# The last step of a fused window-attention and rational-activation kernel: other parts, other engines for its linear terms, another order

## The chip, the cores and the metric

The kernel runs on one core of a Trainium2 chip. The core has engines that run side by side and wait for each other by semaphores: TensorE (PE) multiplies matrices into PSUM, VectorE (DVE) and ScalarE (ACT) work element by element, GpSimd (POOL) and SyncE (SP) here mostly issue DMAs. The metric is the device time of one execution in microseconds (us); lower is better.

## The reference

Attention over a sliding window with four sink keys, then a feed-forward block whose activation is a ratio of polynomials:

```python
scores = scale * q @ k.T                       # 4 batches, 8 heads, 768 rows, 64 wide
keep = is_sink | in_window                     # first 4 keys, or the last 128
x = softmax(where(keep, scores, -1e9)) @ v     # -> 3072 rows, 512 wide
h = x @ w_in                                   # 512 -> 2048
P = a[0] + a[1] * h + a[2] * h2 + a[3] * h3
Q = 1.0 + abs(b[0]) * abs(h) + abs(b[1]) * h2
out = (P / (Q + 1e-06)) @ w_out                # 2048 -> 512
```

## The kernel before

The 3072 rows are worked off in 12 steps of 256 rows (step 0 to 11). In each step TensorE computes scores (`scores`), ScalarE exponentiates them out of PSUM (`exps`), TensorE multiplies with v (`attend`), VectorE divides by the sums (`normalize`), the result is turned (`turn_x`), and the feed-forward part follows on a tile of 128 partitions x 4096 columns: 16 blocks of 128 ff channels ("ff blocks") lie side by side, 256 columns each.

The feed-forward part of a step is made of these pieces, with their lines in the profile:

- `gemm1` (PE, L767): four groups of 4 ff blocks, 16 matmuls each, into a PSUM bank pair called ps_h, ps_o, ps_m; a table `BANK` says which. `copy_in` (ACT, L774) copies a group to hb in bf16 and frees the bank.
- `sqa` / `sqd`: the square (ACT L781 or DVE L783); `and` (DVE L788): the absolute value by a bit mask; `den` (DVE L792): their sum.
- `ln` (ACT L811) and `exp` (ACT L816): the reciprocal of the denominator as exp(-ln). `ln` takes its scale and its bias from one value per partition (`qsc`, `one_eps`).
- `even` (DVE L797): a2*sq + a0; `odd` (DVE L801): a3*sq + a1, in place; `odd_h` (DVE L805): times h; `num` (DVE L808): even + odd_h; `gate` (DVE L821): num times the reciprocal, the input of the second projection.
- `gemm2` (PE, L829): 16 ff blocks x 2 row halves of 128x512 matmuls. `copy_out` (ACT L838; in the last step one half on ACT L567 and one on DVE L569) copies the sums out, `store` (L844, L846) writes them by DMA. Step 10 and those before are stored in one DMA of 512 KB from SP's queue, the last step in two of 256 KB, from ACT's queue and from SP's.

Steps 1 to 10 do the elementwise pieces on all 4096 columns at once. The last step does them in four equal parts of 4 ff blocks (1024 columns), each part with its own two groups of 4 second-projection matmuls, so that TensorE can begin before all of the tile is done. Every engine works off its instructions in the order in which they are written. That order comes from a list of piece numbers, `ORDER`; a negative number there is `spin`, which multiplies a tile of ones on TensorE to no use: `spin(n)` issues n/4 matmuls of 512 columns and the rest as matmuls of 128. `-3` stands before the first scores of step 0.

Of the kernel before, what the change touches and what calls it, by code (L numbers as in the profile page):

```python
# [12 lines left out]
AF = mybir.ActivationFunctionType  # L13
ALU = mybir.AluOpType
# [3 lines left out]
ORDER = [  # L18
# [43 lines left out]
def kernel(  # L62
# [13 lines left out]
    nc = tc.nc  # L76
# [26 lines left out]
    X_PE = 5  # L103
    PARTS0 = 4
    V_PE = 3
    HOLD_X = tuple(range(8))
    HOLD_H = tuple(range(7))
    KB = 3
# [68 lines left out]
             ('gemm1', 9, 1): 'ps_m',  # L177
             ('gemm1', 9, 2): 'ps_o',
             ('gemm1', 9, 3): 'ps_h',
             ('gemm1', 10, 0): 'ps_o',  # L180
             ('gemm1', 10, 1): 'ps_m',
             ('gemm1', 10, 2): 'ps_o',
             ('gemm1', 10, 3): 'ps_m',
             ('gemm1', 11, 0): 'ps_m',
             ('gemm1', 11, 2): 'ps_m',
             ('gemm1', 11, 3): 'ps_m',
             ('gemm2', 6, 0, 0): 'ps_m',
             ('gemm2', 9, 0, 0): 'ps_o',
             ('scores', 0, 0): 'ps_h',
             ('scores', 0, 1): 'ps_m',  # L190
             ('scores', 0, 3): 'ps_m',
# [86 lines left out]
    a0, a1, a2, a3 = (acoef[:, n:n + 1] for n in range(4))  # L278
# [481 lines left out]
    LAST = NSTEP - 1  # L760
# [30 lines left out]
    def denominator(m, c):  # L791
        nc.vector.tensor_tensor(out=den[m][:, c], in0=den[m][:, c], in1=sq[m][:, c], op=ALU.add)  # L792

    def even(m, c):
        if m not in num:
            num[m] = m_sb.tile([P, MW], BF16, tag="num", name="num", bufs=1)
        nc.vector.tensor_scalar(out=num[m][:, c], in0=sq[m][:, c], scalar1=a2, scalar2=a0,  # L797
                                op0=ALU.mult, op1=ALU.add)

    def odd(m, c):  # L800
        nc.vector.tensor_scalar(out=sq[m][:, c], in0=sq[m][:, c], scalar1=a3, scalar2=a1,  # L801
                                op0=ALU.mult, op1=ALU.add)

    def odd_h(m, c):
        nc.vector.tensor_tensor(out=sq[m][:, c], in0=sq[m][:, c], in1=hb[m][:, c], op=ALU.mult)  # L805
# [317 lines left out]

    early_casts = [("cast_k0", 0), ("cast_k0", 1)]

    def cut(n, k_):
        return slice(k_ * MW // n, (k_ + 1) * MW // n)

    def parts(m):
        return 4 if m == LAST else PARTS0 if m == 0 else 1  # L1130

    def every(nm, m):
        return [(nm, m, p_) for p_ in range(parts(m))] if m >= 0 else []
# [1 line left out]
    for m in range(NSTEP):  # L1135
# [15 lines left out]
        if m in HOLD_H:  # L1151
            piece(("hold", "h", m), "POOL", 0.2, r_ + 4, lambda m=m: hold("h", m),
                  [("copy_in", m, j) for j in range(4)])
        w_ = MW // np_
        for p_ in range(np_):
            c = cut(np_, p_)
            js = range(p_ * 4 // np_, (p_ + 1) * 4 // np_)
            ins = [("copy_in", m, j) for j in js]
            d_ = 4.0 * p_ / np_ if np_ > 1 else 3.0
            q_ = 1.2 if m == LAST else 2.5  # L1160
            piece(("and", m, p_), "DVE", on_dve(w_, 4), r_ + d_ + 1.2, lambda m=m, c=c: magnitude(m, c),
                  ins + every("gate", old)
                  + ([("turn_%sc" % w_, s_, g_) for s_ in (1, 2) for w_ in "kq"
                      for g_ in halves(s_, w_)] if m == 1 else []))
            if np_ == 1:
                k_ = SQ_ACT.get(m, 2)
                x_ = k_ * GW
                if k_:
                    piece(("sqa", m, p_), "ACT", on_act(x_), r_ + 3.9,
                          lambda m=m, x_=x_: square(m, slice(0, x_), "act"),  # L1170
                          ins[:k_] + (every("num", old) or early_casts))
                if k_ < 4:
                    piece(("sqd", m, p_), "DVE", on_dve(MW - x_, 2), r_ + 4.25,
                          lambda m=m, x_=x_: square(m, slice(x_, MW), "dve"),
                          ins[k_:] + (every("num", old) or early_casts))
            else:
                eng = "act" if m == LAST or p_ == 0 else "dve"
                nm = "sqa" if eng == "act" else "sqd"
                on = {"act": ("ACT", on_act(w_)), "dve": ("DVE", on_dve(w_, 2))}[eng]
                piece((nm, m, p_), on[0], on[1], r_ + d_ + 1.3,  # L1180
                      lambda m=m, c=c, eng=eng: square(m, c, eng),
                      ins + (every("num", old) or early_casts))
            sqs = [("sqa", m, p_) if ("sqa", m, p_) in work else None,
                   ("sqd", m, p_) if ("sqd", m, p_) in work else None]
            piece(("den", m, p_), "DVE", on_dve(w_, 2), r_ + d_ + 1.4,
                  lambda m=m, c=c: denominator(m, c), [("and", m, p_)] + sqs)
            piece(("ln", m, p_), "ACT", on_act(w_, 0.3), r_ + d_ + 1.8, lambda m=m, c=c: log_den(m, c),
                  [("den", m, p_), ("scalars",)] + every("exp", m - 1))
            piece(("exp", m, p_), "ACT", on_act(w_, 0.2), r_ + d_ + 2.8,
                  lambda m=m, c=c: recip_den(m, c), [("ln", m, p_)])  # L1190
            piece(("even", m, p_), "DVE", on_dve(w_, 3.25), r_ + d_ + 2.6, lambda m=m, c=c: even(m, c),
                  sqs + [("scalars",)]
                  + (every("gate", m - 1) or [("cast_q0", 0), ("cast_q0", 1)]))
            piece(("odd", m, p_), "DVE", on_dve(w_, 3.4), r_ + d_ + 2.8, lambda m=m, c=c: odd(m, c),
                  [("even", m, p_), ("den", m, p_)])
            piece(("odd_h", m, p_), "DVE", on_dve(w_, 2), r_ + d_ + 3.0, lambda m=m, c=c: odd_h(m, c),
                  [("odd", m, p_)])
            piece(("num", m, p_), "DVE", on_dve(w_, 2), r_ + d_ + 3.2,
                  lambda m=m, c=c: numerator(m, c), [("odd_h", m, p_)])
            piece(("gate", m, p_), "DVE", on_dve(w_, 2), r_ + d_ + (3.4 if m == LAST else 6.0),  # L1200
                  lambda m=m, c=c: gate(m, c),
                  [("num", m, p_), ("exp", m, p_)]
                  + ([("gemm2", m - 2, tt, 1) for tt in range(NTS)] if m >= 2 else
                     [("turn_k0", 0), ("turn_k0", 1), ("turn_q0", 0), ("turn_q0", 1)]))
        n2 = 4 if m == LAST else 2
        for tt in range(NTS):
            if m == LAST or tt == 0:
                home = bank_of(("gemm2", m, tt, 0), "ps_m" if m == LAST and tt == 0 else "ps_h")
            for part in range(n2):
                f0, f1 = part * NFFC // n2, (part + 1) * NFFC // n2  # L1210
                gates = [("gate", m, p_) for p_ in range(np_)
                         if p_ * NFFC // np_ < f1 and (p_ + 1) * NFFC // np_ > f0]
                piece(("gemm2", m, tt, part), "PE", 3.48 / n2,
                      (r_ + 10.6 + 2 * tt + part) if m < LAST else (r_ + 8 + part + 0.5 * tt),
                      lambda m=m, tt=tt, f0=f0, f1=f1, home=home: project_out(m, tt, f0, f1, home),
                      gates + [("load_w_out", c) for c in range(f0 * 4 // NFFC, (f1 * 4 + NFFC - 1) // NFFC)]
                      + ([("gemm2", m, tt, part - 1)] if part else [("gemm2", m, 0, 0)] if tt and m < LAST else []),
                      takes=home if part == 0 and (tt == 0 or m == LAST) else None)
# [49 lines left out]
```

## Time and profile before

| | |
|---|---|
| median of 3 runs | 242.64 us (241.71 to 242.86) |
| the profiled execution, its own time | 240.56 us |
| span of the profiled execution, first to last instruction | 238.9 us |
| TensorE busy | 216.1 us, 90% |
| VectorE busy | 215.2 us, 90% |
| ScalarE busy | 210.1 us, 88% |
| GpSimd busy | 92.7 us, 39% |

The time of a run holds some 1.7 us around the span (240.56 less 238.9). All starts below count from the start of the span. Three engines are busy for about nine tenths of it, so no share of busy time alone says which one sets the end; that is read from the waits in each stretch.

### The profile page before, as it was taken

What the parts mean: (1) busy time and instruction counts of PE and PEld (TensorE: products, weight loads), DVE (VectorE), ACT (ScalarE), POOL (GpSimd) and SP (SyncE); (2) the same over time, 40 slices, a digit from 0 to 9 for tenths busy, and PEclk for the clock granted to TensorE, in tenths of its full rate; (3) what the DMA queues carried; (4) which work ended last, traced back from release to release, by engine and by line L of the source; (5) the groups of instructions that cost most, each with busy time, mean ns of one, the idle gap of its engine ahead of it and who ended that gap; (6) DMA issues with size and microseconds to landing.
All of it is one profiled execution on the core that took longest, in us unless ns stands there. A gap on an engine that the chain in (4) does not pass through costs nothing.

```text
span 238.9 us, 7308 instructions
## 1 busy us (share of the span) xinstructions
PE 216.1 (90%) x3229; PEld 146.8 (61%) x3249; DVE 215.2 (90%) x253; ACT 210.1 (88%) x172; POOL 92.7 (39%) x126
## 2 busy tenths in 40 slices
PE   0497898995999999999999999999999999999993
PEld 0365676784874757746578658568647768545431
DVE  3678299999799999898999999999999999999991
ACT  2357799997899998999999899999999999999960
POOL 8914409597939880499910980000000000000000
PEclk9999999999999999999999999999999999999999
DMA  6999999999999999799994999570305110004222
GB/s 186 166 178 137 202 170 79 125 134 128 164 185 147 137 162 150 208 98 77 141 129 89 158 89 73 140 125 26 25 3 198 25 25 0 1 3 170 93 88 88
DMA packets 95375, 26.98 MB, mean 113 GB/s; under 512 B 86128, under 2 KB 92272, under 8 KB 95344
## 3 DMA queue, kind: packets, MB, share of 16 engines
q0 software_dynamic: 65024, 12.98, 84.8%
q1 hardware_dynamic: 28792, 12.61, 28.4%
q10 hardware_dynamic: 1528, 0.93, 1.4%
q8 instruction: 25, 0.41, 0.8%
q14 instruction: 6, 0.05, 0.1%
HBM read 27.30 MB, written 6.29 MB: 141 GB/s over the span
## 4 chain that ended last, share of the span: by engine, by line
PE 52%; ACT 24%; DVE 7%; DMA 6%; issue 4%; POOL 4%; SPq 2%; ACTq 0%; POOLq 0%; DVEq 0%
PE ps_h L829 18%; PE ps_o L767 9%; PE ps_m L767 8%; ACT lnq L811 6%; ACT hb L774 5%; ACT den L816 4%; DMA kT<-k_bf 4%; PE ps_m L829 3%; ACT sq L781 3%; ACT e L667 3%; PE ps_h L767 2%; DMA v<-in_v_dram 2%; PE ps_m L708 2%; PE ps_s L647 1%; SPq L602 1%
## 5 line engine op out<-in xcount | busy, mean ns | idle before, releaser
L767 PEld LDWEIGHTS <-w_in_sb 128*128 128x128 bf16 x768 | 73.7, 98 | 14.8 <-issue 3.5
L829 PE MATMUL ps_h<-w_out_sb,g 128*128 128x512 bf16 x287 | 68.2, 379 | 1.9 <-issue 1.0
L829 PEld LDWEIGHTS <-g 128*128 128x128 bf16 x384 | 36.6, 98 | 42.0 <-DVE g L821 1.6
L811 ACT ACTIVATE lnq<-den,one_eps,qsc 128x4096 f32<-128x4096 bf16 (+1 forms) x18 | 48.2, 2678 | 0.0
L816 ACT ACTIVATE den<-lnq 128x4096 bf16<-128x4096 f32 (+1 forms) x18 | 44.8, 2491 | 0.2
L767 PE MATMUL ps_m<-xblk,w_in_sb 128*128 128x256 bf16 x352 | 42.1, 273 | 0.6 <-ACT hb L774 0.3
L767 PE MATMUL ps_o<-xblk,w_in_sb 128*128 128x256 bf16 x336 | 40.2, 273 | 0.0
L381 POOL DMA_DIRECT2D v<-in_v_dram x48 | 36.1, 765 | 0.1
L808 DVE TENSOR_TENSOR num<-num,sq 128x4096 bf16<-128x4096 bf16 (+1 forms) x18 | 28.3, 1578 | 0.2
L821 DVE TENSOR_TENSOR g<-num,den 128x4096 bf16<-128x4096 bf16 (+1 forms) x18 | 28.3, 1574 | 0.1
L805 DVE TENSOR_TENSOR sq<-sq,hb 128x4096 bf16<-128x4096 bf16 (+1 forms) x18 | 28.3, 1576 | 0.1
L792 DVE TENSOR_TENSOR den<-den,sq 128x4096 bf16<-128x4096 bf16 (+1 forms) x18 | 28.2, 1574 | 0.1
L774 ACT ACTIVATE hb<-ps_o 128x1024 bf16<-128x1024 f32 x21 | 21.8, 1038 | 3.3 <-PE ps_o L767 3.2
L774 ACT ACTIVATE hb<-ps_m 128x1024 bf16<-128x1024 f32 x22 | 22.9, 1039 | 0.6 <-PE ps_m L767 0.5
L667 ACT ACTIVATE e<-ps_s 128x768 bf16<-128x768 f32 (+1 forms) x25 | 22.1, 885 | 0.0
L781 ACT ACTIVATE sq<-hb 128x1024 bf16<-128x1024 bf16 (+1 forms) x15 | 20.1, 1355 | 0.1
L797 DVE TENSOR_SCALAR num<-sq,acoef 128x4096 bf16<-128x4096 bf16 (+1 forms) x18 | 18.3, 1024 | 0.4 <-ACT sq L781 0.3
L801 DVE TENSOR_SCALAR sq<-sq,acoef 128x4096 bf16<-128x4096 bf16 (+1 forms) x18 | 17.9, 999 | 0.2
L783 DVE TENSOR_TENSOR sq<-hb 128x2048 bf16<-128x2048 bf16 (+2 forms) x13 | 16.9, 1300 | 1.0 <-ACT hb L774 0.9
L708 PEld LDWEIGHTS <-e 64*64 64x64 bf16 x1216 | 13.1, 107 | 5.4 <-issue 4.4
L343 POOL DMA_DIRECT2D q_bf<-in_q_dram x15 | 14.8, 988 | 3.7 <-DMA w_out_sb<-in_moe_w_out_dram 3.5
L788 DVE TENSOR_SCALAR den<-hb 128x2048 uint32<-128x2048 uint32 (+1 forms) x18 | 16.1, 896 | 0.0
(136 smaller groups left out, 265.8 us busy)
## 6 DMA issues: line engine op xcount, KB each, us to landing
out_dram<-o_t SPq DMA_DIRECT2D x11, 512.0 KB, 3.0
w_in_sb<-in_moe_w_in_dram POOLq DMA_DIRECT2D x4, 512.0 KB, 10.8
k_bf<-in_k_dram POOLq DMA_DIRECT2D x16, 128.0 KB, 6.2
w_out_sb<-in_moe_w_out_dram POOLq DMA_DIRECT2D x4, 512.0 KB, 8.8
q_bf<-in_q_dram POOLq DMA_DIRECT2D x15, 128.0 KB, 6.2
v<-in_v_dram POOLq DMA_DIRECT2D x24, 64.0 KB, 5.8
stage_v<-in_v_dram POOLq DMA_DIRECT2D x3, 256.0 KB, 9.8
v<-in_v_dram POOLq DMA_DIRECT2D x24, 32.0 KB, 5.0
```

What stands on the lines that cost most here:

```text
L381: nc.gpsimd.dma_start(out=v_fix[b % 2][half(r), g * NHF:(g + steps) * NHF, hl, 0:D], in_=v[b, h, g * TS:(g + steps) * TS, :].rearrange("(j ...
L667: nc.scalar.activation(out=data, in_=ps[:, :, c0:512], func=AF.Exp, scale=inv_sqrt_d)
L767: nc.tensor.matmul(ps[:, n, :], lhsT=w_in_all[:, c, fc * P:(fc + 1) * P], rhs=xblk[m][:, c, :], start=(c == 0), stop=(c == NDMC - 1))
L774: nc.scalar.activation(out=hb[m][:, j * GW:(j + 1) * GW], in_=ps_h.pop((m, j)).rearrange("p n c -> p (n c)"), func=AF.Copy)
L781: nc.scalar.activation(out=sq[m][:, c], in_=hb[m][:, c], func=AF.Square)
L792: nc.vector.tensor_tensor(out=den[m][:, c], in0=den[m][:, c], in1=sq[m][:, c], op=ALU.add)
L805: nc.vector.tensor_tensor(out=sq[m][:, c], in0=sq[m][:, c], in1=hb[m][:, c], op=ALU.mult)
L808: nc.vector.tensor_tensor(out=num[m][:, c], in0=num[m][:, c], in1=sq[m][:, c], op=ALU.add)
L811: nc.scalar.activation(out=lnq_fix[:, c], in_=den[m][:, c], func=AF.Ln, scale=qsc, bias=one_eps)
L816: nc.scalar.activation(out=den[m][:, c], in_=lnq_fix[:, c], func=AF.Exp, scale=-1.0)
L821: nc.vector.tensor_tensor(out=g_of[m][:, c], in0=num[m][:, c], in1=den[m][:, c], op=ALU.mult)
L829: nc.tensor.matmul(ps_out[own][:, tt, :], lhsT=g_of[m][:, co:co + P], rhs=w_out_all[:, fc, :], start=(fc == 0), stop=(fc == NFFC - 1))
```

## The change

The last step is cut into parts of 5, 5, 4 and 2 ff blocks (1280, 1280, 1024 and 512 columns) in place of 4, 4, 4 and 4, for the elementwise pieces and for the second projection alike. For its last two parts the two linear terms, `even` and `odd`, are no longer a VectorE multiply-add but a ScalarE activation with the function Identity, whose scale and bias are the same one value per partition. Some PSUM banks of steps 9 to 11 are exchanged. `ORDER` is another one from the first projection of step 11 on, and the spin at the start is 7 in place of 3.

```diff
 ORDER = [
 ...
-    130, 178, -3, 182, 150, 184, 183, 131, 185, 120, 151, 132, 24, 186, 152, 180, 18, 187, 181, 17,
+    130, 178, -7, 150, 182, 184, 183, 131, 120, 151, 185, 132, 24, 186, 152, 180, 18, 187, 181, 17,
...
+    LAST_FC = (5, 5, 4, 2)
+    TERMS_ACT = (("even", 2), ("odd", 2), ("even", 3), ("odd", 3))
...
-    def even(m, c):
+    def linear(eng, out, in_, slope, shift):
+        if eng == "ACT":
+            nc.scalar.activation(out=out, in_=in_, func=AF.Identity, scale=slope, bias=shift)
+        else:
+            nc.vector.tensor_scalar(out=out, in0=in_, scalar1=slope, scalar2=shift, op0=ALU.mult,
+                                    op1=ALU.add)
+
+    def even(m, c, eng="DVE"):
         if m not in num:
             num[m] = m_sb.tile([P, MW], BF16, tag="num", name="num", bufs=1)
-        nc.vector.tensor_scalar(out=num[m][:, c], in0=sq[m][:, c], scalar1=a2, scalar2=a0,
-                                op0=ALU.mult, op1=ALU.add)
-
-    def odd(m, c):
-        nc.vector.tensor_scalar(out=sq[m][:, c], in0=sq[m][:, c], scalar1=a3, scalar2=a1,
-                                op0=ALU.mult, op1=ALU.add)
+        linear(eng, num[m][:, c], sq[m][:, c], a2, a0)
+
+    def odd(m, c, eng="DVE"):
+        linear(eng, sq[m][:, c], sq[m][:, c], a3, a1)
...
+    def ff_cut(m, n, k_):
+        if m == LAST:
+            return sum(LAST_FC[:k_]), sum(LAST_FC[:k_ + 1])
+        return k_ * NFFC // n, (k_ + 1) * NFFC // n
```

Up to the first `gemm1` group of step 11 the engines run the same instructions in the same order as before, the spin excepted. Then, on TensorE, the four `gemm1` groups of step 11 stand in one row ahead of the second projections of steps 8 and 9; before, two of the four stood among those. On SP's queue the stores of steps 7, 8 and 9 are exchanged. The last instructions of ScalarE change as follows. Before, the place is from the second `copy_out` from the end on (L838 on ps_o is that of step 9, on ps_h that of step 10; L811 is `ln`, L816 `exp`, 1024 columns a part):

```order
L838 ACTIVATE o_t<-ps_o 128x1024
L816 ACTIVATE den<-lnq 128x1024
L811 ACTIVATE lnq<-den,one_eps,qsc 128x1024
L816 ACTIVATE den<-lnq 128x1024
L838 ACTIVATE o_t<-ps_h 128x1024
L811 ACTIVATE lnq<-den,one_eps,qsc 128x1024
L816 ACTIVATE den<-lnq 128x1024
L567 ACTIVATE o_t<-ps_m 128x512
L844 DMA out_dram<-o_t 128x512
```

In the changed kernel, from the `ln` of the second part on (the lines are 7 higher: L818 is `ln`, L823 `exp`, L845 `copy_out` of step 10; L798 is the new Identity):

```order
L818 ACTIVATE lnq<-den,one_eps,qsc 128x1280
L798 ACTIVATE sq<-sq,acoef 128x1024
L823 ACTIVATE den<-lnq 128x1280
L818 ACTIVATE lnq<-den,one_eps,qsc 128x1024
L823 ACTIVATE den<-lnq 128x1024
L798 ACTIVATE sq<-sq,acoef 128x512
L818 ACTIVATE lnq<-den,one_eps,qsc 128x512
L823 ACTIVATE den<-lnq 128x512
L845 ACTIVATE o_t<-ps_h 128x1024
L569 ACTIVATE o_t<-ps_o 128x512
L851 DMA out_dram<-o_t 128x512
```

Step 10's `copy_out` has moved from before the last `ln` to behind the last `exp`, directly ahead of the last step's own `copy_out`, and the two `odd` terms stand among the last `ln` and `exp`. On VectorE the end before was this, from the `odd` of the third part on (L801 `odd`, L805 `odd_h`, L797 `even`, L808 `num`, L821 `gate`):

```order
L801 TENSOR_SCALAR sq<-sq,acoef 128x1024
L821 TENSOR_TENSOR g<-num,den 128x1024
L805 TENSOR_TENSOR sq<-sq,hb 128x1024
L797 TENSOR_SCALAR num<-sq,acoef 128x1024
L808 TENSOR_TENSOR num<-num,sq 128x1024
L801 TENSOR_SCALAR sq<-sq,acoef 128x1024
L821 TENSOR_TENSOR g<-num,den 128x1024
L805 TENSOR_TENSOR sq<-sq,hb 128x1024
L808 TENSOR_TENSOR num<-num,sq 128x1024
L821 TENSOR_TENSOR g<-num,den 128x1024
L569 COPY o_t<-ps_h 128x512
```

In the changed kernel, from the `odd_h` of the second part on (L812 `odd_h`, L815 `num`, L828 `gate`):

```order
L812 TENSOR_TENSOR sq<-sq,hb 128x1280
L815 TENSOR_TENSOR num<-num,sq 128x1280
L828 TENSOR_TENSOR g<-num,den 128x1280
L812 TENSOR_TENSOR sq<-sq,hb 128x1024
L815 TENSOR_TENSOR num<-num,sq 128x1024
L828 TENSOR_TENSOR g<-num,den 128x1024
L812 TENSOR_TENSOR sq<-sq,hb 128x512
L815 TENSOR_TENSOR num<-num,sq 128x512
L828 TENSOR_TENSOR g<-num,den 128x512
L571 COPY o_t<-ps_m 128x512
```

Each part now runs through in one piece, `odd_h`, `num`, `gate`, with no linear term between them.

## Rows read from the trace of the kernel before

**Rows 1.** The page: busy time and its share of the span.

```profile
PE 216.1 (90%) x3229; PEld 146.8 (61%) x3249; DVE 215.2 (90%) x253; ACT 210.1 (88%) x172; POOL 92.7 (39%) x126
```

**Rows 2.** Timeline of TensorE, last 20 us: start, us, instruction, [idle before, releaser].

```profile
219.96 7.07 PE L829 MATMUL ps_h<-w_out_sb,g 128*128 128x512 bf16 x31
227.18 1.04 PE L829 MATMUL ps_m<-w_out_sb,g 128*128 128x512 bf16 x4
228.41 1.02 PE L829 MATMUL ps_h<-w_out_sb,g 128*128 128x512 bf16 x4 [0.20 <-ACT o_t L838]
...
233.08 1.04 PE L829 MATMUL ps_h<-w_out_sb,g 128*128 128x512 bf16 x4 [0.19 <-DVE g L821]
233.95 1.03 PE L829 MATMUL ps_m<-w_out_sb,g 128*128 128x512 bf16 x4
```

**Rows 3.** Timeline of ScalarE and its DMA queue, last 27 us.

```profile
212.83 3.62 ACT L816 ACTIVATE den<-lnq 128x4096 bf16<-128x4096 f32 x1
216.35 1.00 ACT L838 ACTIVATE o_t<-ps_h 128x1024 f32<-128x1024 f32 x1
...
218.16 1.06 ACT L781 ACTIVATE sq<-hb 128x1024 bf16<-128x1024 bf16 x1
219.11 1.24 ACT L811 ACTIVATE lnq<-den,one_eps,qsc 128x1024 f32<-128x1024 bf16 x1
220.24 1.05 ACT L781 ACTIVATE sq<-hb 128x1024 bf16<-128x1024 bf16 x1
...
227.36 1.00 ACT L838 ACTIVATE o_t<-ps_h 128x1024 f32<-128x1024 f32 x1
228.26 1.23 ACT L811 ACTIVATE lnq<-den,one_eps,qsc 128x1024 f32<-128x1024 bf16 x1
229.53 1.06 ACT L816 ACTIVATE den<-lnq 128x1024 bf16<-128x1024 f32 x1
235.02 0.60 ACT L567 ACTIVATE o_t<-ps_m 128x512 f32<-128x512 f32 x1 [4.43 <-PE ps_m L829]
235.65 0.36 ACTq L844 DMA_DIRECT2D out_dram<-o_t  x1
```

**Rows 4.** Timeline of VectorE, the last step.

```profile
220.53 1.00 DVE L797 TENSOR_SCALAR num<-sq,acoef 128x1024 bf16<-128x1024 bf16 x2
...
232.33 0.69 DVE L821 TENSOR_TENSOR g<-num,den 128x1024 bf16<-128x1024 bf16 x1
234.16 0.69 DVE L569 COPY o_t<-ps_h 128x512 f32<-128x512 f32 x1 [1.13 <-PE ps_h L829]
```

**Rows 5.** Timeline of SP's queue, last 13 us: the stores of steps 10 and 11.

```profile
228.39 0.37 SPq L846 DMA_DIRECT2D out_dram<-o_t  x1
234.87 0.34 SPq L844 DMA_DIRECT2D out_dram<-o_t  x1
```

**Rows 6.** Windows: engines' busy time, granted clock, DMA share, GB/s moved (last column).

```profile
229.00:229.50 0.50, 0.50 (x5) 0.20 (x3) 0.50 (x2) 0.50 (x1) 0.00 (x0) 1.00 0.41 156
229.50:230.00 0.50, 0.50 (x4) 0.27 (x3) 0.50 (x2) 0.47 (x1) 0.00 (x0) 1.00 1.04 393
...
237.00:237.50 0.50, 0.00 (x0) 0.00 (x0) 0.00 (x0) 0.00 (x0) 0.00 (x0) 1.00 0.45 168
```

**Rows 7.** Timeline of TensorE around the spin (L614).

```profile
12.78 0.50 PE L614 MATMUL ps_s<-warm 128*128 128x128 bf16 x3
...
14.58 1.06 PE L551 MATMUL ps_o<-ident,stage_d 128*64 128x128 bf16 x16
...
15.89 0.43 PE L655 MATMUL ps_m<-nege,ident 64*64 64x256 bf16 x4
...
16.91 0.30 PE L655 MATMUL ps_h<-nege,ident 64*64 64x256 bf16 x4
...
18.34 0.64 PE L551 MATMUL ps_h<-ident,stage_d 128*64 128x128 bf16 x16 [0.39 <-ACT e L667]
```

**Rows 8.** The chain that ended last, first 60 us: start, us, what.

```profile
12.85 0.43 PE ps_s L614 x3
...
17.27 1.02 ACT e L667
```

More of the change, by code (lines that the diff above doesn't have):

```diff
@@ L179 @@
              ('gemm1', 9, 3): 'ps_h',
-             ('gemm1', 10, 0): 'ps_o',
-             ('gemm1', 10, 1): 'ps_m',
+             ('gemm1', 10, 0): 'ps_m',
              ('gemm1', 10, 2): 'ps_o',
              ('gemm1', 10, 3): 'ps_m',
-             ('gemm1', 11, 0): 'ps_m',
-             ('gemm1', 11, 2): 'ps_m',
-             ('gemm1', 11, 3): 'ps_m',
+             ('gemm1', 11, 1): 'ps_m',
+             ('gemm1', 11, 2): 'ps_o',
              ('gemm2', 6, 0, 0): 'ps_m',
-             ('gemm2', 9, 0, 0): 'ps_o',
+             ('gemm2', 9, 0, 0): 'ps_m',
+             ('gemm2', 11, 0, 0): 'ps_o',
+             ('gemm2', 11, 1, 0): 'ps_m',
              ('scores', 0, 0): 'ps_h',
@@ L1124 @@
     early_casts = [("cast_k0", 0), ("cast_k0", 1)]
-    def cut(n, k_):
-        return slice(k_ * MW // n, (k_ + 1) * MW // n)
+    def ff_cut(m, n, k_):
+        if m == LAST:
+            return sum(LAST_FC[:k_]), sum(LAST_FC[:k_ + 1])
+        return k_ * NFFC // n, (k_ + 1) * NFFC // n
     def parts(m):
-        return 4 if m == LAST else PARTS0 if m == 0 else 1
+        return len(LAST_FC) if m == LAST else PARTS0 if m == 0 else 1
     def every(nm, m):
@@ L1153 @@
                   [("copy_in", m, j) for j in range(4)])
-        w_ = MW // np_
         for p_ in range(np_):
-            c = cut(np_, p_)
-            js = range(p_ * 4 // np_, (p_ + 1) * 4 // np_)
+            f0, f1 = ff_cut(m, np_, p_)
+            w_ = (f1 - f0) * TS
+            c = slice(f0 * TS, f1 * TS)
+            js = range(f0 // GC, -(-f1 // GC))
             ins = [("copy_in", m, j) for j in js]
@@ L1190 @@
                   lambda m=m, c=c: recip_den(m, c), [("ln", m, p_)])
-            piece(("even", m, p_), "DVE", on_dve(w_, 3.25), r_ + d_ + 2.6, lambda m=m, c=c: even(m, c),
+            term = "ACT" if m == LAST and ("even", p_) in TERMS_ACT else "DVE"
+            piece(("even", m, p_), term, on_dve(w_, 3.25), r_ + d_ + 2.6, lambda m=m, c=c, term=term: even(m, c, term),
                   sqs + [("scalars",)]
                   + (every("gate", m - 1) or [("cast_q0", 0), ("cast_q0", 1)]))
-            piece(("odd", m, p_), "DVE", on_dve(w_, 3.4), r_ + d_ + 2.8, lambda m=m, c=c: odd(m, c),
+            term = "ACT" if m == LAST and ("odd", p_) in TERMS_ACT else "DVE"
+            piece(("odd", m, p_), term, on_dve(w_, 3.4), r_ + d_ + 2.8, lambda m=m, c=c, term=term: odd(m, c, term),
                   [("even", m, p_), ("den", m, p_)])
@@ L1204 @@
                      [("turn_k0", 0), ("turn_k0", 1), ("turn_q0", 0), ("turn_q0", 1)]))
-        n2 = 4 if m == LAST else 2
+        n2 = len(LAST_FC) if m == LAST else 2
         for tt in range(NTS):
@@ L1209 @@
             for part in range(n2):
-                f0, f1 = part * NFFC // n2, (part + 1) * NFFC // n2
+                f0, f1 = ff_cut(m, n2, part)
                 gates = [("gate", m, p_) for p_ in range(np_)
-                         if p_ * NFFC // np_ < f1 and (p_ + 1) * NFFC // np_ > f0]
+                         if ff_cut(m, np_, p_)[0] < f1 and ff_cut(m, np_, p_)[1] > f0]
                 piece(("gemm2", m, tt, part), "PE", 3.48 / n2,
```

12 rows, old and new, of the table ORDER are left out of this document.

## The prediction

> **What bounds the kernel now.** I read four views: the page, the timelines of the last 27 us of each engine, the windows over the two stretches in which the last stores move, and the head of the chain that ended last. The page says only that TensorE, VectorE and ScalarE are each busy for 88 to 90% of the span [rows 1], so a share moved from one to another is worth nothing until a stage shows who waits. The tail shows it. TensorE runs the last 64 matmuls of the second projection almost without a stop: 32 of step 10 from 219.96, then 32 of step 11 in groups of four, a group every 0.87 us (233.08 to 233.95) [rows 2]. At that pace 64 take 13.9 us, and would be through at 233.9 plus the 0.16 us by which the last one outlasts its slot, 234.05; the trace has 233.95 + 1.03 = 234.98. So about 0.9 us of waits lie in this tail. They are seen before 227.18 (the first part's gate), before 228.41 (ps_h, until ScalarE has copied step 10 out of it) and before 233.08 (the last gate) [rows 2]. More than 0.9 us of 242.64 the elementwise work cannot win here, since the matmuls themselves are not fewer.
>
> Behind the last matmul come a copy of 0.60 us on ScalarE (235.02), a DMA issue at 235.65 [rows 3], and the data, the last of which move at 237.0 + 168/393 x 0.5 = 237.2 [rows 6]; the span ends at 238.9, 1.65 us later.
>
> ScalarE is the engine to watch. It has no idle time to speak of up to 229.53 + 1.06 = 230.59, and then 4.43 us of idle time before its last copy [rows 3]. VectorE's last gate ends at 232.33 + 0.69 = 233.02 [rows 4] and TensorE's last group starts 0.06 us later.
>
> **The change, part by part.**
>
> *Taken from VectorE.* Two linear terms of 1024 columns, 0.46 us each (two take 1.00 us from 220.53, of which 0.09 is overlap) [rows 4], and two of 512 columns, no dearer: between 1.4 and 1.8 us. With the smaller last part VectorE could end some 2 us sooner. It does not get to: each gate needs the `exp` of its part, and ScalarE has become later (below).
>
> *Given to ScalarE.* No Identity is in the trace, so I bound it. From below by the square, 0.95 us from start to start at 1024 columns (218.16 to 219.11); from above by `ln`, 1.13 (219.11 to 220.24), which like the Identity takes scale and bias from one value per partition [rows 3]. The slope is that of `exp`: 4096 columns take 3.52 (212.83 to 216.35) [rows 3]; a 1024-column `exp` lasts 1.06 as the square does, so 0.95 from start to start; 1024 columns more cost 0.86, and 512 fewer save 0.43. Four terms cost 2 x (0.95 + 0.52) = 2.94 us at the square's price and 2 x (1.13 + 0.70) = 3.66 at that of `ln`. I take 3.66, because the operands are the same, and keep 2.94 for the range.
>
> The Trainium skill ("ScalarE: Activation LUTs", Rules for kernel authors) has multiplies and adds on VectorE, which it calls up to about three times as fast in bf16; the rows here say 0.46 against 0.95 to 1.13, so that rule speaks against the move, and the trace agrees with it.
>
> *The cuts 5, 5, 4, 2.* The same number of squares, `ln`, `exp`, masks and sums over the same 4096 columns: nothing in sum. A fourth part of half the size shortens what follows the last `exp`.
>
> *ScalarE's order.* The same pieces otherwise. An `exp` directly behind its own `ln` starts 1.27 after it (228.26 to 229.53) where 1.13 would do [rows 3]; one such pair fewer saves 0.14. So ScalarE's work, step 10's `copy_out` now the last of it, ends at 230.59 + 3.66 - 0.14 = 234.1. Before, that `copy_out` ended at 227.36 + 1.00 = 228.36, and SP issued its store at 228.39 [rows 3, 5]. **This is the term that decides:** the 512 KB of step 10 now leave 5.7 us later, at 234.1.
>
> *What that store meets.* Before, its data began some 0.9 us after the issue: the half microsecond from 229.0 moved 156 GB/s, which at the full 393 GB/s is its last 0.2 us [rows 6]. At 393 GB/s 512 KB (524 kB) take 1.33 us and 256 KB 0.67. After: issue 234.1, data 235.0 to 236.35. The two last stores come into this. The last `exp` is over at 234.1 - 1.0 = 233.1, the last gate of 512 columns by 233.6, TensorE's last four matmuls (0.87 + 0.16) by 234.7, VectorE's copy of 0.69 [rows 4] by 235.4, and that store's data could begin at 236.3; ScalarE's half is some 0.5 us sooner. Both find the engines taken by step 10's data, so the last byte moves at 236.35 + 2 x 0.67 = 237.7, against 237.2 now: **+0.5 us**. Had step 10's store been out of the way, it would be 236.3 + 0.67 = 237.0, a gain of 0.2: the 0.3 us that TensorE ends sooner less a copy that is 0.1 longer.
>
> By the Trainium skill ("DMA: Bandwidth & Descriptors", Issuing engines are not separate DMA queues) DMAs from any queue interleave on the same 16 engines; by it the sum is +0.5, without it -0.2. No three stores meet in this trace.
>
> *TensorE's order and the banks.* The four `gemm1` groups of step 11 in one row are the same matmuls; the second projections of steps 8 and 9 that come later are waited for by ScalarE only for copies out, behind `exp` of step 10, which lasts to 216.35 in any case [rows 3]. The stores on SP that are exchanged are those of steps 7 to 9, done long before the end. The last step's second half no longer takes ps_h, so the wait before 228.41 goes [rows 2]; in its place the second part's gate waits for an `exp` that is later, some 0.7 us. All this I cost at nothing; if the first copies of step 11 came so late as to hold step 10's `ln`, it would pass one for one into ScalarE's end.
>
> *The spin.* `spin(7)` adds one matmul of 512 columns. The three of 128 take 0.43 us on the chain, 0.143 each [rows 8], so 0.57 at most; a matmul of 512 in the tail takes 0.87/4 = 0.22 [rows 2]. The spin lies where TensorE is still slow: the same 16 transposes take 1.06 us at 14.58 and 0.64 at 18.34, and four matmuls of L655 0.43 at 15.89 and 0.30 at 16.91 [rows 7]; this reads as the lower of its two clock levels (1.2 GHz) up to about 17 and the upper one (2.4 GHz) from there. Twice 0.22 makes 0.43. TensorE is on the chain here, from the spin until ScalarE's `exps` at 17.27 [rows 8], so it passes on. If the rise stays where it is, 0.43 us of work falls behind it and runs in 0.64/1.06 of the time, which gives 0.17 back: **+0.25 us**. Bounds: nothing, if a wait further on absorbs it, and +0.57.
>
> **The sum.** +0.5 + 0.25 = +0.75 on the profiled execution's 240.56 us, 241.3. The median of the runs, 242.64, stands 2.1 us above that execution; the difference carries over, and gives 243.4.
>
> **The rivals.**
>
> *A. The forecast:* step 10's store is last in line, 243.4; with ScalarE's end 0.3 us to either side, 243.0 to 243.8.
>
> *B. Identity is as cheap as the square, and the tail gains.* ScalarE ends 0.72 sooner, at 233.4; step 10's data are through by 235.6, the last by 237.0 or a little before, -0.2 to -0.3. With the spin 242.6: no change. For it: the square's row. Against: `ln` shows what two per-partition operands cost.
>
> *C. The spin brings the clock's rise forward.* The work from the spin to 17.27 is 4 us [rows 8]; at the upper level it would take 0.6 of that, up to 1.6 us less, from which the spin's own 0.4 goes: -1.2. With the tail's +0.5, 241.9; with B's tail 241.2. For it: only the head runs slow, and the added matmul uses all of the array. Against: the transposes and scores before 17 kept TensorE busy too without raising it. The Trainium skill ("TensorE: Matmul & The Clock Gate", Part 1) says that activity is what lifts the throttle and that the moment varies from run to run; that bears on the chance, not on the price.
>
> *D. Slower: the clock rises later than now.* Each microsecond of work that runs at the lower level instead of the upper costs 1.06/0.64 - 1 = 0.65 us more [rows 7]. Since A and the spin give 0.75, it decides (over 1.2 us in all) from 0.7 us of TensorE's work on; at 1.5 us of work it gives +1.75, 244.4. For it: everything behind the spin is shifted, and the runs of before differ by 1.15 us among themselves, which such a shift would explain. Against: there is more work ahead of the rise, not less.
>
> **Chances.** A 0.5, B 0.2, C 0.15, D 0.15. A change of 0.5%, 1.2 us, is about what a measurement of this kernel can tell from none: 241.4 and 243.85 are the bounds. A and B lie inside them but for A's upper edge; C is outside with B's tail; D nearly always. Faster 0.12, same 0.74, slower 0.14. The predicted time is A's. The range leaves out the lower half of C and the upper half of D: 241.5 to 244.4.
>
> **What the changed profile would show.** ScalarE: Identity at 1.2 us (square's price: 1.06) for 1024 columns; no idle time over 0.2 us up to step 10's `copy_out`, which ends near 234 plus the head's shift. SP: step 10's store issued right behind it, and the windows at full rate without a dip from there to the end. TensorE: a wait of some 0.7 us before the last step's second part, none over 0.1 before its last. Head: scores start 0.4 us later, ScalarE's `exps` of 17.27 0.2 to 0.3 later. It would be wrong if step 10's store left early, if stores moved side by side at more than 393 GB/s, or if TensorE's head ran at another speed than now.

## The result, and the profile after

The changed kernel is slower: 242.5 us against 240.87 us (medians of 20 runs each, taken in turn), a ratio of 1.0084 with a 95% interval of [1.0056, 1.0113]. Of 240.87 us that is 2.0 us more, 1.3 to 2.7 by the interval. The forecast was 243.4 us, 0.75 us more than before, in a range of 241.5 to 244.4: the time lies in the range and the sign is right, but the change is more than twice the forecast one, and its interval lies wholly above the 1.2 us that the forecast counted as no change. The medians are over all runs and the ratios over the undisturbed ones; the changed kernel's profiled execution, 244.85 us at a mean granted clock of 0.981, was disturbed in its first 65 us, so tails are compared here and not spans.

To compare tails I need a mark that stands at the same place in both orders: ScalarE's first copy of step 10's projection, right behind `exp` of step 9. Here it is on ScalarE's timeline of the kernel before, and then of the changed one (start, us, instruction):

```profile
203.31 1.01 ACT L774 ACTIVATE hb<-ps_m 128x1024 bf16<-128x1024 f32 x1
```

```profile
205.59 1.01 ACT L776 ACTIVATE hb<-ps_o 128x1024 bf16<-128x1024 f32 x1
```

From the mark to the end of the span it is 238.9 - 203.31 = 35.6 us before and 243.1 - 205.59 = 37.5 after: 1.9 us more, nearly all that the runs show. The page of the changed kernel says nothing of it (compare [rows 1]):

```profile
PE 218.5 (90%) x3231; PEld 148.0 (61%) x3250; DVE 214.4 (88%) x249; ACT 213.7 (88%) x176; POOL 89.8 (37%) x126
```

TensorE's timeline, the last step (answers to [rows 2]):

```profile
231.96 1.25 PE L836 MATMUL ps_o<-w_out_sb,g 128*128 128x512 bf16 x5 [0.50 <-DVE g L828]
233.05 1.24 PE L836 MATMUL ps_m<-w_out_sb,g 128*128 128x512 bf16 x5
...
236.30 0.59 PE L836 MATMUL ps_m<-w_out_sb,g 128*128 128x512 bf16 x2
```

One wait of 0.50 us before the second part, none behind it. TensorE ends at 236.30 + 0.59 = 236.89, 31.30 us from the mark; before it was 234.98 - 203.31 = 31.67. So the matmuls are 0.37 us sooner through, as they were meant to be.

ScalarE's timeline (answers to [rows 3]; L798 is the new Identity, L845 `copy_out`, on ps_h that of step 10):

```profile
225.01 1.25 ACT L798 ACTIVATE num<-sq,acoef 128x1024 bf16<-128x1024 bf16 x1
226.14 1.28 ACT L823 ACTIVATE den<-lnq 128x1280 bf16<-128x1280 f32 x1
...
228.65 1.24 ACT L798 ACTIVATE sq<-sq,acoef 128x1024 bf16<-128x1024 bf16 x1
229.78 1.27 ACT L823 ACTIVATE den<-lnq 128x1280 bf16<-128x1280 f32 x1
...
233.17 0.80 ACT L798 ACTIVATE sq<-sq,acoef 128x512 bf16<-128x512 bf16 x1
233.88 0.80 ACT L818 ACTIVATE lnq<-den,one_eps,qsc 128x512 f32<-128x512 bf16 x1
234.71 0.63 ACT L823 ACTIVATE den<-lnq 128x512 bf16<-128x512 f32 x1
235.25 1.01 ACT L845 ACTIVATE o_t<-ps_h 128x1024 f32<-128x1024 f32 x1
236.50 0.60 ACT L569 ACTIVATE o_t<-ps_o 128x512 f32<-128x512 f32 x1 [0.24 <-PE ps_o L836]
```

ScalarE is busy without a stop, and step 10's copy is over at 236.26, 30.67 us from the mark, where it was 25.05. VectorE's timeline (answers to [rows 4]) shows what follows from that:

```profile
235.37 0.43 DVE L828 TENSOR_TENSOR g<-num,den 128x512 bf16<-128x512 bf16 x1 [0.48 <-ACT den L823]
239.25 0.69 DVE L571 COPY o_t<-ps_m 128x512 f32<-128x512 f32 x1 [3.45 <-DMA out_dram<-o_t]
```

VectorE's last copy takes TensorE's last result out of ps_m, and that result is there at 236.89. The copy starts at 239.25, and what ended the wait is not TensorE but a DMA: a store out of an `o_t` tile. Of the 3.45 us, 239.25 - 236.89 = 2.36 lie behind TensorE's end. SP's queue (answers to [rows 5]) and the chain that ended last (start, us, what) say which store:

```profile
236.28 0.37 SPq L853 DMA_DIRECT2D out_dram<-o_t  x1
239.96 0.34 SPq L851 DMA_DIRECT2D out_dram<-o_t  x1
```

```profile
236.28 2.79 DMA out_dram<-o_t
```

The store of step 10 is issued at 236.28 and lands 2.79 us later, at 239.07; the copy starts 0.18 us behind it, and the last store is issued at 239.96. The pool of `o_t` tiles has two buffers. Step 11 asks for two tiles, one for each half: the first gets the buffer of step 9, the second that of step 10, which is not free until step 10's store has landed. In the windows (columns as in [rows 6]) the DMA engines have nothing to move while the copy runs:

```profile
237.00:237.50 0.50, 0.00 (x0) 0.00 (x0) 0.00 (x0) 0.09 (x1) 0.00 (x0) 1.00 0.64 242
...
239.00:239.50 0.50, 0.00 (x0) 0.00 (x0) 0.25 (x1) 0.00 (x0) 0.00 (x0) 1.00 0.47 172
239.50:240.00 0.50, 0.00 (x0) 0.00 (x0) 0.44 (x1) 0.00 (x0) 0.00 (x0) 1.00 0.00 0
...
241.00:241.50 0.50, 0.00 (x0) 0.00 (x0) 0.00 (x0) 0.00 (x0) 0.00 (x0) 0.50 0.98 373
```

So my case of all the last stores side by side did not come about: step 10's store and ScalarE's half, issued at 237.12, overlap, but by the time the last was issued, at 239.96, both had landed (2.79 us and 2.6 us from issue). The tail adds up: TensorE -0.37; the last copy behind TensorE's end 2.36 instead of 0.04, +2.32; the copy 0.09 longer; from the last issue to the end 243.1 - 239.96 = 3.14 instead of 238.9 - 235.65 = 3.25, -0.1. Together +1.9.

### The profile page after: what moved, and what is told of

The parts are those of the page before. It is cut to its first block, busy times and chain, and to the rows that moved or that the text cites. A ratio compares the mean times of both kernels' runs of the same rounds, so it can differ in the third digit from the quotient of the medians.

```text
span 243.1 us, 7313 instructions
## 1 busy us (share of the span) xinstructions
PE 218.5 (90%) x3231; PEld 148.0 (61%) x3250; DVE 214.4 (88%) x249; ACT 213.7 (88%) x176; POOL 89.8 (37%) x126
## 4 chain that ended last, share of the span: by engine, by line
PE 40%; ACT 26%; DVE 12%; DMA 9%; POOL 4%; issue 4%; SPq 2%; DVEq 0%; POOLq 0%; ACTq 0%
PE ps_h L836 12%; PE ps_o L769 7%; ACT lnq L818 6%; ACT den L823 6%; ACT hb L776 5%; PE ps_m L769 5%; DMA kT<-k_bf 3%; PE ps_m L836 3%; DMA q_bf<-in_q_dram 3%; PE ps_h L769 3%; ACT e L669 3%; ACT sq L783 2%; DVE x_n L719 2%; DMA qT<-q_bf 2%; ACT o_t L845 2%
## 5 line engine op out<-in xcount | busy, mean ns | idle before, releaser
L818 ACT ACTIVATE lnq<-den,one_eps,qsc 128x4096 f32<-128x4096 bf16 (+3 forms) x18 | 48.3, 2681 | 0.0
L823 ACT ACTIVATE den<-lnq 128x4096 bf16<-128x4096 f32 (+3 forms) x18 | 44.8, 2491 | 0.2
L828 DVE TENSOR_TENSOR g<-num,den 128x4096 bf16<-128x4096 bf16 (+3 forms) x18 | 28.3, 1575 | 1.1 <-ACT den L823 0.9
L815 DVE TENSOR_TENSOR num<-num,sq 128x4096 bf16<-128x4096 bf16 (+3 forms) x18 | 28.4, 1576 | 0.3
L812 DVE TENSOR_TENSOR sq<-sq,hb 128x4096 bf16<-128x4096 bf16 (+3 forms) x18 | 28.3, 1575 | 0.2
L794 DVE TENSOR_TENSOR den<-den,sq 128x4096 bf16<-128x4096 bf16 (+3 forms) x18 | 28.3, 1573 | 0.1
L783 ACT ACTIVATE sq<-hb 128x1024 bf16<-128x1024 bf16 (+3 forms) x15 | 20.3, 1359 | 0.1
L836 PE MATMUL ps_m<-w_out_sb,g 128*128 128x512 bf16 x76 | 18.5, 379 | 0.4 <-issue 0.2
L800 DVE TENSOR_SCALAR num<-sq,acoef 128x4096 bf16<-128x4096 bf16 (+2 forms) x16 | 17.2, 1075 | 0.4 <-ACT sq L783 0.3
L800 DVE TENSOR_SCALAR sq<-sq,acoef 128x4096 bf16<-128x4096 bf16 (+2 forms) x16 | 16.9, 1054 | 0.3
```

Of the source, the lines that this page charges most:

```text
L800: nc.vector.tensor_scalar(out=out, in0=in_, scalar1=slope, scalar2=shift, op0=ALU.mult, op1=ALU.add)
L815: nc.vector.tensor_tensor(out=num[m][:, c], in0=num[m][:, c], in1=sq[m][:, c], op=ALU.add)
L818: nc.scalar.activation(out=lnq_fix[:, c], in_=den[m][:, c], func=AF.Ln, scale=qsc, bias=one_eps)
L823: nc.scalar.activation(out=den[m][:, c], in_=lnq_fix[:, c], func=AF.Exp, scale=-1.0)
L828: nc.vector.tensor_tensor(out=g_of[m][:, c], in0=num[m][:, c], in1=den[m][:, c], op=ALU.mult)
L836: nc.tensor.matmul(ps_out[own][:, tt, :], lhsT=g_of[m][:, co:co + P], rhs=w_out_all[:, fc, :], start=(fc == 0), stop=(fc == NFFC - 1))
```

## The experiments

The theory after this reading: **the buffer**, VectorE's last copy waits for step 10's store to leave the tile that it needs. The rivals: **the traffic**, three stores that share the DMA engines (my forecast's reason); **the terms**, four Identities too many on ScalarE; and **the head**, the longer spin. Every kernel was timed in 5 rounds against the kernel before. An interval here is some 0.9% wide, so the ratio alone seldom decides; the tail from the mark, which repeats within 0.1 us, does. The first four were compared with 35 runs of the kernel before (median 241.19 us), the next three with 29 (241.81), the last two with 22 (240.52).

**A tile of its own for the last half.** The wait goes, and everything else stays.

```diff
-            o_t[m, tt] = o_sb.tile([P, NTS, DM], FP32, tag="o_t", name="o_t")[:, tt, :]
+            o_t[m, tt] = (o_sb.tile([P, DM], FP32, tag="o_l", name="o_l", bufs=1) if tt else
+                          o_sb.tile([P, NTS, DM], FP32, tag="o_t", name="o_t")[:, tt, :])
```

> The last half of the output gets an SBUF tile of its own (2 KB a partition), so that VectorE's last copy no longer shares a buffer with step 10's output. Buffer theory (the copy waits until step 10's store has landed): the copy starts within 0.1 us of TensorE's last matmul instead of 2.4 us behind it; the three stores then meet, so some 0.7 us of the 2.4 are given back: 1.6 us faster than the changed kernel, ratio to before 1.002. Traffic theory (the late store costs only by sharing the DMA engines): no change, 1.008. Head theory (the longer spin costs the 2 us): no change, 1.008.

Measured: 240.67 us, ratio 1.0001 [0.9956, 1.0046]. The mark on ScalarE, TensorE's last matmuls, VectorE's last copy, SP's queue and the windows of this kernel:

```profile
202.71 1.01 ACT L776 ACTIVATE hb<-ps_o 128x1024 bf16<-128x1024 f32 x1
```

```profile
233.41 0.59 PE L836 MATMUL ps_m<-w_out_sb,g 128*128 128x512 bf16 x2
```

```profile
234.04 0.69 DVE L571 COPY o_l<-ps_m 128x512 f32<-128x512 f32 x1 [1.13 <-PE ps_m L836]
```

```profile
233.39 0.37 SPq L854 DMA_DIRECT2D out_dram<-o_t  x1
234.76 0.34 SPq L852 DMA_DIRECT2D out_dram<-o_l  x1
```

```profile
234.50:235.00 0.50, 0.00 (x0) 0.00 (x0) 0.23 (x1) 0.00 (x0) 0.00 (x0) 1.00 1.05 393
...
236.50:237.00 0.50, 0.00 (x0) 0.00 (x0) 0.00 (x0) 0.00 (x0) 0.00 (x0) 1.00 1.01 381
```

The last copy now waits for TensorE alone and starts 0.04 us behind its end (233.41 + 0.59 = 234.00). The tail is 238.7 - 202.71 = 36.0 us, 1.5 less than in the changed kernel. This kernel is the one that my forecast described: step 10's store is late, the three stores move one behind the other or side by side at 369 to 393 GB/s, and the last issue is 238.7 - 234.76 = 3.94 us from the end instead of 3.25. So the traffic costs 0.7 us; with TensorE's 0.37 and the 0.09 of the copy the tail stands at +0.4 against before. The traffic is real, and it is the price of a kernel that I had not been given.

**Step 10's copy and store earlier.** The pieces 733 (`copy_out` of step 10) and 734 (its store) are listed ahead of 768, the `ln` of the third part, which puts the copy five instructions earlier on ScalarE:

```diff
-    753, 736, 754, 771, 762, 759, 785, 763, 768, 791, 764, 772, 786, 769, 773, 781, 792, 774, 778,
-    782, 787, 783, 779, 733, 793, 784, 788, 734, 794, 789, 795, 790, 796
+    753, 736, 754, 771, 762, 759, 785, 763, 733, 734, 768, 791,
+    764, 772, 786, 769, 773, 781, 792, 774, 778, 782, 787, 783, 779, 793, 784, 788, 794, 789, 795,
+    790, 796
```

> Step 10's copy out and its store stand before the last step's third ln on ScalarE, three pieces earlier; nothing else moves. Buffer theory: the copy ends 4.3 us sooner, the store lands before TensorE is through, the last copy waits for TensorE alone; the last exps are 0.9 us later and TensorE's end 0.4: 1.9 us faster than the changed kernel, ratio 1.001. Traffic theory: only the 0.5 us of the shared engines comes back, less the 0.4: ratio 1.008. Head theory: 1.008 or a little more.

Measured: 242.38 us, ratio 1.0068 [1.0024, 1.0112]. TensorE's and VectorE's timelines:

```profile
232.04 1.04 PE L837 MATMUL ps_o<-w_out_sb,g 128*128 128x512 bf16 x4 [0.66 <-DVE g L829]
```

```profile
234.92 0.69 DVE L572 COPY o_t<-ps_m 128x512 f32<-128x512 f32 x1 [1.13 <-PE ps_m L837]
```

The wait for the store is gone here too, without another buffer, and the tail is 239.0 - 202.68 = 36.3 us. But the 0.9 us of the copy stand before the last parts' `ln` and `exp`, a gate is 0.66 us late, and TensorE ends at 234.88, 32.20 from the mark, instead of 31.30: 0.9 us later, where I had expected 0.4. The ratio came out higher than I expected, its interval reaches down to 1.0024, and the tail's +0.7 us (1.003) is inside it.

**The spin of 3 in the changed kernel.**

```diff
-    130, 178, -7, 150, 182, 184, 183, 131, 120, 151, 185, 132, 24, 186, 152, 180, 18, 187, 181, 17,
+    130, 178, -3, 150, 182, 184, 183, 131, 120, 151, 185, 132, 24, 186, 152, 180, 18, 187, 181, 17,
```

> The changed kernel with the spin of before (3). Buffer theory: the tail keeps its 2 us; ratio 1.007 by the 0.25 us that I gave to the spin, 1.008 if the spin costs nothing. Head theory: 1.000.

Measured: 242.33 us, ratio 1.0043 [1.0000, 1.0086]. VectorE's timeline:

```profile
235.58 0.69 DVE L571 COPY o_t<-ps_m 128x512 f32<-128x512 f32 x1 [3.45 <-DMA out_dram<-o_t]
```

The same wait to the hundredth, and the tail is 239.5 - 201.93 = 37.6 us. The tail's loss has nothing to do with the spin. The ratio by itself does not say so: its interval takes in both what the buffer gives (1.007) and what the head gives (1.000).

**The four terms back on VectorE.**

```diff
-    TERMS_ACT = (("even", 2), ("odd", 2), ("even", 3), ("odd", 3))
+    TERMS_ACT = ()
```

> The four linear terms of the last two parts are VectorE's again, in the same order; ScalarE has 3.7 us less to do. Buffer theory: step 10's copy ends and its store lands 3.5 us sooner, so the last copy waits for TensorE alone; VectorE's last gate is some 0.5 us later: ratio 1.001 to 1.003. If instead the terms were no part of the loss (head theory): 1.008.

Measured: 241.86 us, ratio 1.0009 [0.9961, 1.0057]. The mark and step 10's copy on ScalarE, and VectorE's last copy:

```profile
206.79 1.02 ACT L776 ACTIVATE hb<-ps_o 128x1024 bf16<-128x1024 f32 x1
...
234.87 1.01 ACT L845 ACTIVATE o_t<-ps_h 128x1024 f32<-128x1024 f32 x1
```

```profile
239.07 0.69 DVE L571 COPY o_t<-ps_m 128x512 f32<-128x512 f32 x1 [1.59 <-PE ps_m L836]
```

Tail 243.1 - 206.79 = 36.3 us. Without the terms ScalarE's copy of step 10 is over 235.88 - 206.79 = 29.09 us from the mark, 1.6 sooner than with them, its store lands in time, and the last copy waits for TensorE alone; but TensorE now ends 32.18 us from the mark, 0.88 later than with them. So the terms on ScalarE do for TensorE's end what they were put there for. What makes the change slow is that its order and the terms together push step 10's copy behind the point from which its buffer is missed: the copy is 4.0 us later than before (29.09 against 25.05) without any term on ScalarE, and 5.6 with them. I had expected 3.5 us sooner and not 1.6; without the terms ScalarE now waits, 1.33 us of it for VectorE's `den` ahead of the second part's `ln`.

**Own tile and spin of 3 together** (the first and the third edit).

> The changed kernel with a tile of its own for the last half of step 11 and with the spin of 3: neither the wait for the buffer nor the longer spin is left. Buffer theory: tail 36.0 us against 35.55 before (three stores side by side, 0.4 us), last VectorE copy waits for TensorE alone, ratio 1.000 to 1.003. If the new parts and the terms on ScalarE were themselves what costs: tail above 37 us, ratio 1.006 or more.

Measured: 241.07 us, ratio 1.0052 [1.0007, 1.0096]; the tail is 237.1 - 201.16 = 35.9 us. The tail is the expected one, and the parts and terms are cleared by it. The ratio is above the 1.000 to 1.003 that I gave, with an interval that still takes in 1.001: by the tail 0.4 us are explained, and the rest of the ratio's middle is not.

**Only the even terms on ScalarE, the early copy, the spin of 3.** This was to keep TensorE's gain and pay no wait for it: the third edit, the second edit, and

```diff
-    TERMS_ACT = (("even", 2), ("odd", 2), ("even", 3), ("odd", 3))
+    TERMS_ACT = (("even", 2), ("even", 3))
```

> The changed kernel with three edits: spin of 3, only the two even terms of the last two parts on ScalarE (the odd ones back on VectorE), and step 10's copy out and store put ahead of the logarithm of step 11's third part. Worked out with the durations of the traces: step 10's copy ends near 26.4 us after the tail's marker, its store lands near 30, TensorE ends at 31.2 to 31.4 (31.67 before), so that nothing waits for the buffer and the tail is 35.2 to 35.6 us against 35.55: ratio 0.998 to 1.001. If the ScalarE terms cost the end by themselves, the tail is above 36.3 us as in the run with the early copy: ratio 1.003 or more.

Measured: 240.26 us, ratio 1.0013 [0.9966, 1.0060]. VectorE's timeline:

```profile
238.97 0.69 DVE L572 COPY o_t<-ps_m 128x512 f32<-128x512 f32 x1 [1.53 <-PE ps_m L837]
```

Tail 243.0 - 207.40 = 35.6 us, that of the kernel before, with TensorE 0.14 us sooner through (31.53 from the mark). So the wait can be avoided, and this version wins nothing by it. Whether another order would have a shorter tail than the kernel before is open.

**The spin of 7 in the kernel before.** The head by itself, in two runs.

```diff
-    130, 178, -3, 182, 150, 184, 183, 131, 185, 120, 151, 132, 24, 186, 152, 180, 18, 187, 181, 17,
+    130, 178, -7, 182, 150, 184, 183, 131, 185, 120, 151, 132, 24, 186, 152, 180, 18, 187, 181, 17,
```

> The kernel before with the spin of 7 matmuls in place of 3 and nothing else, so that the head stands alone. My prediction's term: +0.25 us, ratio 1.001, and the tail from ScalarE's first copy of step 10 to the end of the span stays at 35.6 us, as in the kernel before. Rival: the first copy_in of step 0 came 1.1 us later in two traced runs with 7 than in two with 3, and 0.8 us of it was left where the tail begins; if that belongs to the spin, ratio 1.003 to 1.004. If the clock rises earlier and that pays: below 0.997.

> The kernel before with the spin of 7 once more, on the same chip as the next one. My term of +0.25 us gives ratio 1.001. The head's rival: all five traced runs with 7 had their first copy_in 1.0 to 2.1 us later than the four with 3; if 1 us of it reaches the end, ratio 1.004, and with the first run of this kernel an interval that leaves out 1.001.

Measured: 240.51 us, ratio 1.0006 [0.9963, 1.0050], and 240.76 us, ratio 1.0012 [0.9972, 1.0053]. The first run's traced execution had step 0's first copy at 30.07 us, the second's at 27.95, as the kernel before. One program, 2.1 us apart. TensorE's timeline of the second execution, to be held against [rows 7]:

```profile
14.42 0.64 PE L551 MATMUL ps_o<-ident,stage_d 128*64 128x128 bf16 x16
...
21.13 0.22 PE L708 MATMUL ps_h<-v,e 64*64 64x65 bf16 x3 [1.13 <-issue]
```

With the longer spin the 16 transposes at 14.42 take 0.64 us, where they took 1.06 at 14.58, and TensorE is ahead for a while, as my rival C had it. (The granted clock of the windows reads 1.00 here in both traces, so the level is read off durations: four matmuls of L655 take 0.42 us at 23.17 in the first run, where it reads 0.50, and 0.28 at 22.23 in the second, where it reads 1.00; the head of the kernel before has 0.42 to 0.43 up to 15.89.) Then it stands still for 1.13 us for a reason that the profile doesn't show ("issue"), up to 21.13. That is the time at which the gap of the kernel before ended too, and there it was 0.24:

```profile
21.13 0.22 PE L708 MATMUL ps_h<-v,e 64*64 64x65 bf16 x2 [0.24 <-issue]
```

So what the faster head gives is lost in this gap. That it is the spin that makes the head faster is not shown: of the four traced executions with the spin of 3, two have it too. TensorE's timeline of the changed kernel with the spin of 3:

```profile
14.32 0.64 PE L553 MATMUL ps_o<-ident,stage_d 128*64 128x128 bf16 x16 [0.24 <-DVE kT L571]
...
21.16 0.22 PE L710 MATMUL ps_h<-v,e 64*64 64x65 bf16 x2 [0.99 <-issue]
```

In the first run's execution the gap was 1.35 us and ended at 21.39, and from within it on the granted clock lay at the lower level, 0.50 (windows):

```profile
20.00:22.00 2.00, 0.65 (x19) 0.60 (x18) 0.58 (x3) 0.00 (x0) 1.57 (x3) 0.66 1.38 137
22.00:24.00 2.00, 2.00 (x37) 1.09 (x30) 0.69 (x1) 1.37 (x2) 2.00 (x4) 0.50 0.96 131
```

That is where its 2.1 us went. It doesn't come each time: with the spin of 7 four traced executions of six have the lower level somewhere between 19 and 28 us (the other two are this second run and the kernel with its own tile), with the spin of 3 none of four.

**A spin of 19 in the kernel before.**

```diff
-    130, 178, -3, 182, 150, 184, 183, 131, 185, 120, 151, 132, 24, 186, 152, 180, 18, 187, 181, 17,
+    130, 178, -19, 182, 150, 184, 183, 131, 185, 120, 151, 132, 24, 186, 152, 180, 18, 187, 181, 17,
```

> The kernel before with a spin of 19, four matmuls of 512 columns and three of 128, in place of three of 128: twelve more 128-column pieces than with 7. If each added matmul of 512 columns passes on 0.25 us, as my term has it: +1.0 us, ratio 1.004; at most 4 x 0.43 less nothing, +1.7 us, 1.007. If the head keeps 1 us for the first added matmul and as much for each further: +4 us, 1.017. If what comes behind is held by something at a fixed time (TensorE's issue gap that ended at 21.1 to 21.4 us in every trace), little of it shows at the first copy_in: below 1.003.

Measured: 241.19 us, ratio 1.0016 [0.9974, 1.0057]. TensorE's timeline:

```profile
12.76 2.06 PE L614 MATMUL ps_s<-warm 128*128 128x512 bf16 x7
...
22.42 0.28 PE L708 MATMUL ps_h<-v,e 64*64 64x65 bf16 x6 [1.36 <-issue]
```

The spin takes 2.06 us, 1.56 more than the 0.50 of [rows 7], and its gap ends 1.29 us later than before. Of that the whole run shows 0.4 us (-0.6 to +1.4). A cost of 1 us for each added matmul of 512 columns, 4 us here, is ruled out; my 0.25 each, 1.0 in all, is not.

## Why the prediction was right in its time and wrong in its mechanism

**The time** of 242.5 us lies inside 241.5 to 244.4, and that is luck. The forecast added 0.75 us to a median of 242.64; in the runs taken in turn the kernel before had 240.87, and from there it would have been 241.6. The change itself, 2.0 us, is above the 1.76 by which the range reaches over 242.64 (its interval takes that in), and above the 1.2 us that stood for "same", which had a chance of 0.74.

**The step that failed** is the price of the term that it called the one that decides, step 10's late store: "Both find the engines taken by step 10's data ... **+0.5 us**". It saw rightly that step 10's copy becomes ScalarE's last work and that its store leaves 5.7 us later (5.6 from the mark, 30.67 against 25.05). But it asked of the late store only whom it meets on the DMA engines, and not who waits for it to land. The tile is shared: the last half's copy needs the buffer that this store reads, so it starts 2.36 us behind TensorE's end instead of 0.04. The term was +0.5; the tail measured +1.9, and giving that copy another buffer took 1.5 of it back (37.5 to 36.0). With the buffer out of the way the tail's +0.4 is about the +0.5 that was forecast, as the run with its own tile shows.

The rows ahead of the prediction could have told it. Two buffers were there before too, and step 10's store was issued at 228.39 [rows 5]. The page's list of DMA issues (what, queue, count, size, median us from issue to landing) had the rest:

```profile
out_dram<-o_t SPq DMA_DIRECT2D x11, 512.0 KB, 3.0
```

So the buffer was free by some 231.4, and TensorE's end, behind which it is written again (by ScalarE's half in that order), was at 234.98 [rows 2]: 3.6 us of slack. A store 5.7 us later, as forecast, overdraws them by 2.1, and the 0.3 us by which TensorE was to end sooner makes it 2.4 us, against the 2.36 measured. That sum needed a question and no new number.

**ScalarE's price** was right. From start to start an Identity of 1024 columns takes 1.13 us (225.01 to 226.14, 228.65 to 229.78), one of 512 takes 0.71 (222.05 to 222.76, 233.17 to 233.88): 3.7 us for four, against 3.66. Rival B, the square's price, falls. The rule that I cited from the Trainium skill ("ScalarE: Activation LUTs", Rules for kernel authors), multiplies and adds on VectorE, holds for the single instruction here (1.13 us against 0.46). It does not tell what a move is worth in this stage: with the terms back on VectorE TensorE ended 0.88 us later, and yet the tail was 1.2 us shorter (36.3 against 37.5), since the wait for the buffer went with them.

**TensorE's end** was right: 0.3 us sooner forecast, 0.37 measured; a wait of 0.7 us before the second part forecast, 0.50 measured, and none before the last.

**The stores' traffic** was right in size where it happened: three stores close together in the run with its own tile, 369 to 393 GB/s with no dip, 0.7 us to the end, as the forecast had it (237.7 against 237.0); the Trainium skill's rule ("DMA: Bandwidth & Descriptors", Issuing engines are not separate DMA queues) agrees with those windows. In the changed kernel the three did not all meet.

**The spin** at +0.25 us: the two runs of it alone give +0.15 and +0.3 us with intervals of about a microsecond to either side, so the number is neither shown nor refuted. Its reasoning was wrong in part. I had ScalarE's `exps` of 17.27 [rows 8] 0.2 to 0.3 us later; ScalarE's timeline of the changed kernel has them sooner:

```profile
16.91 1.02 ACT L669 ACTIVATE e<-ps_h 128x1024 bf16<-128x1024 f32 x1
```

That is the sign of being wrong that it had named, TensorE's head at another speed. The faster head (rival C) paid nothing, since TensorE then stands longer in the issue gap near 21 us; and it need not come of the spin: with the spin of 3 the `exps` start at 17.27 and 17.37 in two traced executions, at 16.23 and 16.07 in the other two. The forecast took one execution's head for the kernel's. Rival D's change, +1.75 us, is near the measured one, by another cause: the tail is as much longer with the spin of 3 (37.6 against 35.6).

**Open:** what decides in an execution how soon TensorE's head is fast; what TensorE waits for in the issue gap near 21 us; and why the ratio of the run with its own tile and the spin of 3 has its middle at 1.0052 when its tail says 1.001.

## What to carry to other kernels

When a change makes a store late, ask first which tile it reads and who writes into that buffer next, and compare the store's landing with that writer's start; the bandwidth that it shares comes second. Moving an instruction to the end of an engine's queue moves the freeing of everything that it and its DMA hold: of the buffer here, by 5.6 us together with the terms added ahead of it, with 3.6 us of slack. And measure a tail from a mark inside the trace: here it repeated within 0.1 us, where 20 runs of the kernel before lay between 238.0 and 244.0.

## What the runs showed of the hardware that was not expected

Much of the spread between the traced executions has one place. Near 56 us TensorE's scores need kT, which comes by a DMA, and in six of the eleven traced executions it waited for it, for 1.76 to 3.74 us, in five not at all, whatever the kernel and the spin; the spin of 7 in the kernel before shows both, 2.50 us in one run and none in the other. TensorE's timeline of the kernel before, and of the one with the even terms:

```profile
59.02 0.36 PE L647 MATMUL ps_m<-qT,kT 64*64 64x192 bf16 x8 [2.44 <-DMA kT<-k_bf]
```

```profile
60.34 0.36 PE L650 MATMUL ps_m<-qT,kT 64*64 64x192 bf16 x8 [3.74 <-DMA kT<-k_bf]
```

Behind such a wait the granted clock fell to the lower level, 0.50, for some 3 us in four of the six executions, here in the changed kernel's windows, after a wait of 1.88 us, and not in others (1.00 throughout in the kernel before, after 2.44 us):

```profile
59.00:61.00 2.00, 1.49 (x17) 0.92 (x18) 1.79 (x2) 0.98 (x2) 2.00 (x3) 0.67 4.22 78
61.00:63.00 2.00, 2.00 (x11) 1.42 (x10) 2.00 (x1) 0.01 (x1) 2.00 (x4) 0.50 1.77 146
```

From step 0's first copy to the mark the five executions without the wait take 173.4 to 174.2 us, the two with the wait alone 175.4 and 175.9, the four with the fall behind it 176.6 to 179.5. So a wait with its fall costs up to 5.5 us: the even-terms kernel had its first copy at 27.95 us and its mark at 207.40, the changed kernel with the spin of 3, which did not wait, 27.97 and 201.93.
